# A fused routed-attention and two-MLP kernel: first transfers spread over two queues, weight steps moved later by slots, a finished row of w3 @ w_out closed in three slots

## The chip, the cores and the metric

One core of one Trainium2 chip. The metric is the device time of one execution in microseconds (us), from several executions of the same program; before the change its median is 868.74 us (3 runs, 865.44 to 872.73).

## The reference, cut to what matters

```python
# attention: B, H, S, D = 2, 8, 768, 64; 16 clusters
q_n, k_n, c_n = each divided by (its norm over D + 1e-6)
q_assign = argmax(einsum('bhsd,hcd->bhsc', q_n, c_n), -1)      # the same for k_assign
scores = where(q_assign == k_assign, q @ k.T / sqrt(D), -1e9)
attn = exp(scores - max(scores)); attn = attn / (sum(attn) + 1e-9)
x = attn @ v                      # -> (1536, 512)
# first MLP, w1 and w2 (512, 1024), w3 (1024, 1024), w_out (1024, 512)
x = (((x @ w1) * (x @ w2)) @ w3) @ w_out
# second MLP, w_in (512, 2048), w_out2 (2048, 512)
out = softplus(x @ w_in) @ w_out2
```

The weights arrive as 64-bit floats. Products are made of three single-precision passes (high part, low part), so that they come out near full precision.

## The kernel before, in words

Attention works on 16 heads in 8 pairs. A head's scores are handled in six **slots**, so that the attention loop has 96 slots, and 10 more in which the last slots are finished. Slot s does, in this order on every engine: `mx_pe(s)`, two matmuls (L597, tile `mb`) for a block of 128 queries, and `mx_red(s)` (L606, VectorE, tile `mn`), which takes their extreme; nine slots later `st_pe` (L627, tile `sb`) and `st_exp` (L634, ScalarE, tile `E`), and one slot later still `av_pe` (L642, tile `avb`). So one row of L606 stands for one slot, and the trace has 96 of them.

Two other pieces of work are threaded through the slots by hand:

- **The preparation of the next pair.** The tables `PE` and `EV` give each step a place relative to the pair's first slot (12 times the pair's number): load q and k (`load_qk`, tile `rawqk`, L198), square them (`norm_sq`; on ScalarE for pairs 0 and 1, on GpSimd from pair 2), fold the squares (`norm_fold`, GpSimd, L263), sum them (`norm_sum`, VectorE, L271), transpose (`t1_pe`, L304), split into high and low parts (`t1_ev`: ScalarE writes `H` at L315, VectorE writes `L` at L316), find the clusters (`sims_*`, `assign`), copy `H` and `L` into the heads' operands `q` and `k` (`t_dma`, L332 to L337, seven transfers for each head on SP's queue), and add the cluster rows (`back_*` gives tile `sg`, which `m_dma`, L419, copies). `H` and `L` have one buffer for the first and one for the second head of a pair, so that the third `t1_ev` of a pair (14 slots before the pair's first) cannot write `H_1` until the transfers out of the last pair's `H_1` (4 slots before that pair's first) have landed.
- **The product w3 @ w_out.** It is made beforehand, in 24 pieces (8 of `w_out`, 16 of `w3`, in two rounds g = 0 and 1). Piece n begins at step 3n, and `w_step(k, kinds)` does everything that is due at step k by the table `WT`: `A` scale (L63), `b` `c` `d` the bit operations that turn 64-bit words into floats (L462, L466, L471), `s` split a piece of `w_out` (tiles `woh`, `wol`), `T` transpose a piece of `w3` (L493), `h` `l` its high and low parts, `m` twelve matmuls (L512), `p` add the first round's result (L520, VectorE; nothing in round 0), `q` write the result (ScalarE, `w3oh`), `e` its low part (VectorE in round 1). `d` also issues the load of a later piece (`w_load`, L81). The counter `wk` is the next step; the 82nd ends the work, and then `feed.load(3)` issues the first three pieces of `w1` and `w2` (tile `w12r`, 512 KB each).

Before the loop, pair 0 is prepared, pair 1 as far as `t1_ev`, and `wk` reaches 14. So slot s does step 14 + s: the last `m` is at slot 62, and `feed.load(3)` stands at the end of slot 67. All loads before the loop are on SP's queue: centroids, q and k of pair 0, three pieces of weights, v of pair 0, then (behind the 14 transfers of `t_dma`) q, k and v of pair 1. Three banks of PSUM (`rbank`) pass between all these steps by `take` and `give`; `ring` has two buffers for `sq`, `sT` and `sg`.

After the loop both MLPs run (L789, L811, L989, L1032); nothing there is touched.

Of the kernel before, what the change touches and what calls it, by code (L numbers as in the profile page):

```python
# [8 lines left out]
F32 = mybir.dt.float32  # L9
# [9 lines left out]
P = 128  # L19
# [3 lines left out]
def f32(ap):  # L23
    return ap.bitcast(F32)
# [3 lines left out]
def fused_kernel(ctx: ExitStack, tc, q, k, v, centroids, w1, w2, w3, wo, w_in, w_o2, out):  # L28
# [6 lines left out]
    nc = tc.nc  # L35
    B, H, S, D = q.shape
# [3 lines left out]
    QC = S // P  # L40
# [9 lines left out]
    def pool(es, name, bufs=1, side="left", space=None):  # L50
        kw = dict(name=name, bufs=bufs, reuse_waits="tile")
        if space is not None:
            kw["space"] = space
        if space != DRAM:
            kw["side"] = side
        return es.enter_context(tc.tile_pool(**kw))
# [15 lines left out]
    dma_in = nc.sync.dma_start  # L72
# [43 lines left out]
            )  # L116
        return outs

    nc.scalar.preload_act_table_set("natural_log_exp_and_others")
    identF = cpool.tile([P, P], F32, name="identF")  # L120
    make_identity(nc, identF)
    identB = cpool.tile([P, P], BF16, name="identB")
# [56 lines left out]
    ap1 = pool(es_prep, "ap1")  # L179
# [8 lines left out]

    QK, QT, KT, V, PR = {}, {}, {}, {}, {}

    def load_qk(pi):
        if pi >= NPAIR:
            return
        b, h0 = divmod(2 * pi, H)
        r = ap1.tile([P, 2, QC, 2, D], F32, tag="rawqk", name=f"rawqk{pi}")
        for ni, src in enumerate((q, k)):
            for j in range(2):
                dma_in(r[:, j, :, ni, :], src[b, h0 + j].rearrange("(p c) d -> p c d", p=P))  # L198
        QK[pi] = r

    def centroid_load():
        PR["cw"] = ap1.tile([P, D], F32, name="cw")
        dma_in(PR["cw"], centroids.rearrange("h c d -> (h c) d"))
# [54 lines left out]
        PR["sq", j] = sq  # L258

    def norm_fold(pi, j):  # L260
        sq = PR["sq", j]
        for w in (32, 16):
            nc.gpsimd.tensor_tensor(  # L263
                out=sq[..., :w], in0=sq[..., :w], in1=sq[..., w : 2 * w], op=ALU.add
            )

    def norm_sum(pi, j):
        if j == 0:
            PR["n"] = ap1.tile([P, 4, QC, 2, 2], F32, tag="nrm", name=f"nrm{pi}")
        w = 16 if pi else D  # L270
        nc.vector.tensor_reduce(  # L271
            out=PR["n"][:, 0, :, :, j], in_=PR["sq", j][..., :w], op=ALU.add, axis=AX.X
        )
# [139 lines left out]
        nc.scalar.activation(sg, PR["bk"][:, :S], AF.Copy, scale=bigcol[:, 0:1])  # L413
        give(PR["bm"])

    def m_dma(pi, j):
        for ni, d in enumerate((QT, KT)):
            o = 64 * ni + 32 * j
            nc.sync.dma_start(f32(d[2 * pi + j][96:, 0, :]), f32(PR["sg"][o : o + 32, :]))  # L419

# [6 lines left out]
    NW = len(wseq)  # L429
# [103 lines left out]
    def w3_end(n):  # L533
# [7 lines left out]

    WT = {
        "o": {0: "Ab", 1: "c", 2: "d", 5: "s"},
        "3": {0: "Ab", 1: "c", 2: "d", 3: "T", 4: "hl", 7: "m", 8: "pq", 9: "e"},
    }
    WF = {
        "A": w_scale, "b": lambda n: w_bits(n, 0), "c": lambda n: w_bits(n, 1),
# [4 lines left out]
    def w_step(k, kinds):  # L552
        for n in range(max(0, k // 3 - 3), min(NW, k // 3 + 1)):
            for x in WT[wseq[n][0]].get(k - 3 * n, ""):
                if x in kinds:
                    WF[x](n)
# [3 lines left out]
    def load_v(pi):  # L560

        if pi < NPAIR:
            b, h0 = divmod(2 * pi, H)
            for j in range(2):
                t = xp.tile([P, QC, 2 * D], F32, tag="x", name=f"v{pi}_{j}")
                nc.gpsimd.memset(t[:, :, D * (1 - j) : D * (2 - j)], 1.0)
                dma_in(
                    t[:, :, D * j : D * j + D], v[b, h0 + j].rearrange("(p c) d -> p c d", p=P)
                )
                V[2 * pi + j] = t  # L570
# [16 lines left out]
    NH = B * H  # L587
    NSLOT = NH * QC
    ML = 9
    AL = 1  # L590
# [90 lines left out]
    def x_norm(u):  # L681
        g, hf = divmod(u, 2)
        b, h = divmod(g, H)
        if b not in XT:
            XT[b] = xp_.tile([P, CC, S], F32, tag="x1", name="xT1")
        rs = slice(D * (h % 2), D * (h % 2) + D)
        cs = slice(hf * HALF, (hf + 1) * HALF)
        nc.gpsimd.tensor_tensor(  # L688
            out=XT[b][rs, h // 2, cs],
            in0=TT.pop(u)[rs], in1=R[g // 2][rs, cs], op=ALU.mult,  # L690
        )
# [138 lines left out]


    WALL = "AbcdsThlmpqe"
    W0 = 14
    wk = [0]

    def w_next(kinds=WALL):
        w_step(wk[0], kinds)
        wk[0] += 1

    with tc.manual_schedule():  # L840
        centroid_load()
        load_qk(0)
        for _ in range(3):
            w_load()
        load_v(0)
        centroid_prep()
        t1_pe(0, 0)
        t1_pe(0, 1)
        t1_ev(0, 0)
        norm_sq(0, 0)  # L850
        t1_ev(0, 1)
        centroid_turn()
        t1_pe(0, 2)
        t1_pe(0, 3)
        t1_ev(0, 2)
        norm_sq(0, 1)
        t1_ev(0, 3)
        t_dma(0, 0)
        t_dma(0, 1)
        load_qk(1)  # L860
        load_v(1)
        norm_sum(0, 0)
        sims_pe(0, 0)
        sims_ev(0, 0)
        norm_sum(0, 1)
        norm_root(0)
        sims_pe(0, 1)
        sims_ev(0, 1)
        w_next()
        norm_rec(0, 0)  # L870
        norm_rec(0, 1)
        simsT_pe(0)
        w_next()
        norm_rec(0, 2)
        w_next()
        assign(0, 0)
        assign(0, 1)
        w_next()
        back_pe(0)
        back_ev(0)  # L880
        m_dma(0, 0)
        m_dma(0, 1)
        for r in range(-20, -2 * QC):
            steps(PE, r + 2 * QC)
            steps(EV, r + 2 * QC)
            if wk[0] < W0:
                w_next()
        while wk[0] < W0:
            w_next()
        for s in range(NSLOT + ML + AL):  # L890
            j = s - ML
            a = j - AL
            if s < NSLOT:
                mx_pe(s)
                mx_red(s)
            if s and s % QC == 0 and s <= NSLOT:
                m_row(s // QC - 1)
            w_step(wk[0], "hlpqe")
            if a > 0 and a % 3 == 0:
                av_ev(a // 3 - 1)  # L900
            steps(PE, s)
            steps(EV, s)
            if 0 <= j < NSLOT:
                st_pe(j)
                st_exp(j)
            w_step(wk[0], "Abcds")
            if 0 <= a:
                av_pe(a)
            w_step(wk[0], "Tm")
            wk[0] += 1  # L910

            for g in range(NH):
                r = s - (ML + AL + QC * g + QC - 1)
                if r in (2, 4, 6):
                    r_ev(g, r // 2 - 1)
                if r == 8:
                    x_norm(2 * g)
                    x_norm(2 * g + 1)
            if wk[0] == NWSTEP:
                feed.load(3)  # L920
                assert s < ML + AL + QC * NH // 2 + QC + 6
            if s == NSLOT + 1:
                feed.take(2)
                taken += 2
# [176 lines left out]
```

## Time and profile before

| what | value |
|---|---|
| median of 3 runs | 868.74 us (865.44 to 872.73) |
| the profiled execution | 863.85 us, of which the span of the core is 862.0 us |
| busy share of the span | TensorE 93%, VectorE 57%, ScalarE 46%, GpSimd 28% |
| granted TensorE clock, mean | 0.976 of full speed |

The span runs from the first to the last instruction; the remaining 1.85 us lie around it. PE is TensorE (PEld its weight loads), DVE is VectorE, ACT is ScalarE, POOL is GpSimd, SP is the engine that only issues transfers. "L606" is line 606 of the kernel before. In a row of the timeline the bracket holds the idle time of the engine ahead of the row and what ended it.

### The profile page before, as it was taken

The numbers are of one execution on the slowest core, as the hardware profiler recorded it, in microseconds if no ns is written. First come the engines' busy times: TensorE is split into PE (matmuls) and PEld (weight loads), VectorE is DVE, ScalarE is ACT, GpSimd is POOL, SyncE is SP. The second block draws the span as 40 slices with busy tenths as digits, with TensorE's granted clock in tenths as the row PEclk, the third lists the DMA queues.
The fourth block names the chain that finished last, engine by engine and source line by source line (L and its number), as shares of the span: only waits on it lengthen the run. The fifth ranks groups of instructions, "written<-read, shape, count | busy, mean of one in ns | idle before, by whom it ended". The sixth has DMA issues, their size and how long they took to land.

```text
span 862.0 us, 10099 instructions
## 1 busy us (share of the span) xinstructions
PE 797.6 (93%) x3553; PEld 634.6 (74%) x3553; DVE 493.4 (57%) x823; ACT 398.0 (46%) x683; POOL 244.6 (28%) x233
## 2 busy tenths in 40 slices
PE   3279999899989799989999999999999999999997
PEld 3167777677868577757888888888877788888886
DVE  6595566676764545547652345563988744454442
ACT  3425455544453344465453334454564644455443
POOL 2340314442414021125411113231444222222222
PEclk9589999999999989999999999999999999999999
DMA  9775446664633825125511113340120010001001
GB/s 224 163 196 128 129 121 155 155 171 107 145 84 81 195 47 124 35 59 169 184 57 41 58 49 127 117 146 1 49 74 1 7 43 1 0 1 49 1 1 49
DMA packets 77827, 76.40 MB, mean 89 GB/s; under 512 B 46416, under 2 KB 62928, under 8 KB 77776
## 3 DMA queue, kind: packets, MB, share of 16 engines
q1 hardware_dynamic: 77776, 75.75, 33.0%
q8 instruction: 28, 0.46, 0.2%
q14 instruction: 23, 0.19, 0.1%
HBM read 50.41 MB, written 3.24 MB: 62 GB/s over the span
## 4 chain that ended last, share of the span: by engine, by line
PE 74%; DVE 10%; DMA 6%; issue 3%; ACT 3%; SPq 2%; POOL 1%; ACTq 0%; POOLq 0%; DVEq 0%
PE avb L642 11%; PE rb L789 8%; PE sb L789 8%; PE sb L627 7%; PE sb L989 6%; PE mb L1032 6%; PE rb L989 5%; PE rb L512 4%; PE mb L811 4%; PE mb L597 3%; PE rb L1032 3%; PE avb L1032 3%; DMA k<-H 2%; PE avb L811 2%; PE rb L811 2%
## 5 line engine op out<-in xcount | busy, mean ns | idle before, releaser
L606 DVE TENSOR_REDUCE mn<-mb 128x1 f32<-128x768 f32 x96 | 91.6, 954 | 104.1 <-PE mb L597 103.8
L642 PE MATMUL avb<-E,v 128*128 128x384 f32 x384 | 141.9, 491 | 0.0
L66 POOL TENSOR_TENSOR u<-u,t 128x512 f32<-128x512 f32 x48 | 68.4, 1426 | 170.8 <-DVE u L1012 166.6
L627 PE MATMUL sb<-q,k 128*128 128x384 f32 (+1 forms) x384 | 90.4, 357 | 20.8 <-ACT E L634 20.8
L634 ACT ACTIVATE E<-sb 128x768 f32<-128x768 f32 x96 | 77.7, 809 | 49.1 <-PE sb L627 48.4
L642 PEld LDWEIGHTS avb<-E,v 128*128 128x128 f32 x384 | 71.9, 192 | 27.7 <-issue 1.2
L627 PEld LDWEIGHTS sb<-q,k 128*128 128x128 f32 (+1 forms) x384 | 66.4, 192 | 28.2 <-ACT E L634 25.9
L597 PE MATMUL mb<-k,q 128*128 128x384 f32 x192 | 67.9, 435 | 13.1 <-DVE mn L606 13.0
L989 PE MATMUL sb<-ys,wh_i 128*128 128x512 f32 x192 | 64.1, 395 | 3.5 <-ACT t L1000 2.3
L989 PE MATMUL rb<-ys,wh_i 128*128 128x512 f32 x192 | 63.4, 392 | 0.0
L789 PE MATMUL rb<-xs,wh 128*128 128x512 f32 x192 | 61.7, 392 | 0.0
L789 PE MATMUL sb<-xs,wh 128*128 128x512 f32 x192 | 61.6, 392 | 0.0
L1002 DVE TENSOR_SCALAR u<-t 128x512 f32<-128x512 f32 x48 | 21.1, 440 | 67.7 <-ACT t L1001 67.7
L597 PEld LDWEIGHTS mb<-k,q 128*128 128x128 f32 x192 | 34.6, 192 | 33.9 <-DVE mn L606 18.6
L66 POOL TENSOR_TENSOR wl_o<-d_o,wh_o 128x512 fp32r<-128x512 f32 x16 | 21.6, 1352 | 120.8 <-ACT wh_o L61 120.8
L69 DVE TENSOR_TENSOR gl<-u,gh 128x512 fp32r<-128x512 f32 x48 | 39.6, 825 | 19.6 <-ACT gh L61 19.2
L688 POOL TENSOR_TENSOR xT<-t,R 64x384 f32<-64x384 f32 x32 | 34.2, 1086 | 50.8 <-DMA R<-rd 50.6
L1011 ACT ACTIVATE u<-u 128x512 f32<-128x512 f32 x48 | 30.4, 633 | 35.7 <-DVE t L1008 35.6
L989 PEld LDWEIGHTS sb<-ys,wh_i 128*128 128x128 f32 x192 | 35.9, 188 | 13.6 <-ACT t L1000 3.4
L989 PEld LDWEIGHTS rb<-ys,wh_i 128*128 128x128 f32 x192 | 36.1, 188 | 8.0
L789 PEld LDWEIGHTS rb<-xs,wh 128*128 128x128 f32 x192 | 36.1, 188 | 7.9
L789 PEld LDWEIGHTS sb<-xs,wh 128*128 128x128 f32 x192 | 36.1, 188 | 7.8
(175 smaller groups left out, 1773.9 us busy)
## 6 DMA issues: line engine op xcount, KB each, us to landing
w3r<-in_moe_w_dram SPq DMA_DIRECT2D x16, 512.0 KB
w12r<-in_moe_w_dram SPq DMA_DIRECT2D x16, 512.0 KB
wir<-in_moe_w_in_dram SPq DMA_DIRECT2D x16, 512.0 KB
wor<-in_moe_w_out_dram SPq DMA_DIRECT2D x16, 512.0 KB
q<-H SPq DMA_DIRECT2D x16, 384.0 KB
w3r<-in_moe_w_out_dram SPq DMA_DIRECT2D x8, 512.0 KB
rawqk<-in_q_dram SPq DMA_DIRECT2D x16, 192.0 KB
rawqk<-in_k_dram SPq DMA_DIRECT2D x16, 192.0 KB
```

What stands on the lines that cost most here:

```text
L66: nc.gpsimd.tensor_tensor(out=o, in0=i, in1=hi, op=ALU.subtract)
L69: return nc.vector.tensor_tensor(out=o, in0=i, in1=hi, op=ALU.subtract)
L512: nc.tensor.matmul(m, a[:, ks], bb, start=(mc == 0 and x == 0), stop=(mc == NK - 1 and x == 2))
L597: nc.tensor.matmul(mbank[:, hf, :HALF], QT[g][:, 0, c * P : (c + 1) * P], KT[g][:, 0, hf * HALF : (hf + 1) * HALF], start=True, stop=True,)
L606: nc.vector.tensor_reduce(out=MN[g][:, c : c + 1], in_=mbank[:, :, :HALF], op=ALU.min, axis=AX.XY)
L627: nc.tensor.matmul(sbank[:, i, :HALF], KT[g][: P - 31 * n, n, ks], QT[g][: P - 31 * n, n, qs], start=(n == 0), stop=(n == 1),)
L634: nc.scalar.activation(E[j], sbank[:, :, :HALF], AF.Exp, scale=-1.0)
L642: nc.tensor.matmul(avbank[:, :HALF], V[g][:, 2 * kp + i, :], e[:, i, :], start=(kp == 0 and i == 0), stop=(kp == 2 and i == 1),)
L789: nc.tensor.matmul(bk[:, :BLK], a[:, sl], bb, start=(n == 0), stop=(n == 3 * CC - 1))
L811: nc.tensor.matmul(ybank[e][:, :BLK], a[:, es], bb, start=(fc == 0 and n == 0), stop=(fc == NFC - 1 and n == 2),)
L989: nc.tensor.matmul(hbank[(bl * NF2 + fc) % 4][:, :BLK], a[:, sl], bb, start=(n == 0), stop=(n == 3 * CC - 1))
L1032: nc.tensor.matmul(ob, a[:, sl], bb, start=(fc == 0 and n == 0), stop=(fc == NF2 - 1 and n == 2),)
```

## The change

Three edits. (1) The q and k of pair 0 go by head: the first head's on SP's queue ahead of the centroids, the second head's on ScalarE's queue, ahead of ScalarE's table load; q and k of pair 1 and the `m_dma` of pair 0 are issued by ScalarE; v of pairs 0 and 1 are loaded last before the loop; pair 1's squares are no longer folded on GpSimd but summed in full width by VectorE. (2) The decoding before the loop ends at step 12, and no step is done in slots 0 to 5, so that slot s does step 6 + s. (3) `p` and `q` stand at steps 8 and 9 instead of both at 8, and `e` at 10 instead of 9.

```diff
-    nc.scalar.preload_act_table_set("natural_log_exp_and_others")
...
-    def load_qk(pi):
+    def load_qk(pi, js=range(2), dma=dma_in):
...
-        for ni, src in enumerate((q, k)):
-            for j in range(2):
-                dma_in(r[:, j, :, ni, :], src[b, h0 + j].rearrange("(p c) d -> p c d", p=P))
-        QK[pi] = r
+        if js[0] == 0:
+            QK[pi] = ap1.tile([P, 2, QC, 2, D], F32, tag="rawqk", name=f"rawqk{pi}")
+        for j in js:
+            for ni, src in enumerate((q, k)):
+                dma(
+                    QK[pi][:, j, :, ni, :], src[b, h0 + j].rearrange("(p c) d -> p c d", p=P)
+                )
...
     def norm_fold(pi, j):
+        if pi < 2:
+            return
...
-        w = 16 if pi else D
+        w = 16 if pi >= 2 else D
...
-    def m_dma(pi, j):
+    def m_dma(pi, j, dma=dma_in):
...
-            nc.sync.dma_start(f32(d[2 * pi + j][96:, 0, :]), f32(PR["sg"][o : o + 32, :]))
+            dma(f32(d[2 * pi + j][96:, 0, :]), f32(PR["sg"][o : o + 32, :]))
...
-        "3": {0: "Ab", 1: "c", 2: "d", 3: "T", 4: "hl", 7: "m", 8: "pq", 9: "e"},
+        "3": {0: "Ab", 1: "c", 2: "d", 3: "T", 4: "hl", 7: "m", 8: "p", 9: "q", 10: "e"},
...
-    W0 = 14
+    W0 = 12
...
+        act_dma = nc.scalar.dma_start
+        load_qk(0, [0])
+        load_qk(0, [1], act_dma)
+        nc.scalar.preload_act_table_set("natural_log_exp_and_others")
         centroid_load()
-        load_qk(0)
...
-        load_v(0)
...
-        load_qk(1)
-        load_v(1)
...
-        w_next()
+        load_qk(1, dma=act_dma)
...
-        m_dma(0, 0)
-        m_dma(0, 1)
+        m_dma(0, 0, act_dma)
+        m_dma(0, 1, act_dma)
...
-            if wk[0] < W0:
+            if r % 2 == 0:
+                w_next()
                 w_next()
         while wk[0] < W0:
             w_next()
+        load_v(0)
+        load_v(1)
...
-            w_step(wk[0], "hlpqe")
+            weights = s >= QC
+            if weights:
+                w_step(wk[0], "hlpqe")
...
-            w_step(wk[0], "Tm")
-            wk[0] += 1
+            if weights:
+                w_step(wk[0], "Tm")
+                wk[0] += 1
```

(The steps `Abcds` stand under the same condition.) What the instructions look like now at three places:

SP's queue from the program's start, before (`rawqk` is q and k as loaded, `cw` the centroids, `w3r` a piece of weights; a name's last number is a buffer; "waits DMAHW2" is a wait until the last transfer that used that semaphore has landed):

```order
L203 DMA cw<-in_centroids_dram 128x64
L198 DMA rawqk_149<-in_q_dram 128x6x64 x2
L198 DMA rawqk_149<-in_k_dram 128x6x64 x2
L81 DMA w3r_154<-in_moe_w_out_dram 128x1024
L81 DMA w3r_156<-in_moe_w_out_dram 128x1024
L81 DMA w3r_158<-in_moe_w_out_dram 128x1024
L567 DMA v_0_160<-in_v_dram 128x6x64 [waits DMAHW0_49]
L567 DMA v_1_163<-in_v_dram 128x6x64 [waits DMAHW1_49]
L332 DMA q_215<-H_0_178 64x2x768 [waits DMAHW2_49,Activation_49]
```

ScalarE's queue now, behind the eviction of the clusters' scores (`sT`) of pair 0, up to the squares of pair 1 (`sq_0_284`, `sq_1_291`):

```order
L198 DMA rawqk_246<-in_q_dram 128x6x64 [waits DMAHW5_49]
L198 DMA rawqk_246<-in_k_dram 128x6x64 [waits DMAHW7_49]
L198 DMA rawqk_246<-in_q_dram 128x6x64 [waits DMAHW1_49]
L198 DMA rawqk_246<-in_k_dram 128x6x64 [waits DMAHW3_49]
L63 ACTIVATE w3r_154<-w3r_154 128x512
L416 ACTIVATE sg_278<-rb_102,bigcol 128x768 [waits PE_49]
L422 DMA q_209<-sg_278 32x768 [waits DMAHW6_49,Activation_49]
L422 DMA k_210<-sg_278 32x768 [waits DMAHW0_49]
L422 DMA q_219<-sg_278 32x768 [waits DMAHW2_49]
L422 DMA k_220<-sg_278 32x768 [waits DMAHW4_49]
L258 ACTIVATE sq_0_284<-rawqk_246 128x768 [waits DMAHW7_49,DMAHW5_49]
L258 ACTIVATE sq_1_291<-rawqk_246 128x768 [waits DMAHW3_49,DMAHW4_49,DMAHW2_49,DMAHW6_49,DMAHW1_49,DMAHW0_49]
```

Before, none of these transfers was on ScalarE's queue; they stood on SP's, the loads of pair 1 behind all fourteen transfers of `t_dma`. The second square waits for six semaphores: two of its own loads and the four transfers out of `sg`, whose buffer it takes over.

SP's queue around `feed.load(3)`, before (`w12r` is a piece of w1 or w2; the rows behind it are the `m_dma` and `t_dma` of pair 6):

```order
L672 DMA rd_2379<-r_2330 128x6
L81 DMA w12r_0_2381<-in_moe_w_dram 128x4x256
L81 DMA w12r_1_2383<-in_moe_w_dram 128x4x256
L81 DMA w12r_0_2385<-in_moe_w_dram 128x4x256
L419 DMA q_2291<-sg_2365 32x768
L419 DMA k_2292<-sg_2365 32x768
L332 DMA q_2397<-H_1_2113 64x2x768
L333 DMA k_2398<-H_1_2113 64x768
```

and now (the rows behind it are the first head's `t_dma` of pair 7, the last pair):

```order
L675 DMA rd_2523<-r_2470 128x6
L679 DMA R_2411<-rd_2523 64x768
L81 DMA w12r_0_2559<-in_moe_w_dram 128x4x256
L81 DMA w12r_1_2561<-in_moe_w_dram 128x4x256
L81 DMA w12r_0_2563<-in_moe_w_dram 128x4x256
L658 DMA sd_2497<-t_2568 1x384
L335 DMA q_2575<-H_0_2359 64x2x768
L336 DMA k_2576<-H_0_2359 64x768
```

The three loads of `w12r` stood ahead of transfers out of `H_1` that a later write of `H_1` waits for; they now stand behind the last such write.

## Rows read from the trace of the kernel before

**Rows 1.** The page: busy us, share of the span and instructions

```profile
PE 797.6 (93%) x3553; PEld 634.6 (74%) x3553; DVE 493.4 (57%) x823; ACT 398.0 (46%) x683; POOL 244.6 (28%) x233
```

**Rows 2.** Timeline of VectorE: start us, us, what; slots 0, 12, 24, 36, 48, 60, 72

```profile
42.79 0.95 DVE L606 TENSOR_REDUCE mn<-mb 128x1 f32<-128x768 f32 x1
...
78.71 0.96 DVE L606 TENSOR_REDUCE mn<-mb 128x1 f32<-128x768 f32 x1 [2.47 <-PE mb L597]
...
125.02 0.96 DVE L606 TENSOR_REDUCE mn<-mb 128x1 f32<-128x768 f32 x1 [2.16 <-PE mb L597]
...
167.43 0.96 DVE L606 TENSOR_REDUCE mn<-mb 128x1 f32<-128x768 f32 x1 [1.69 <-PE mb L597]
...
213.09 0.96 DVE L606 TENSOR_REDUCE mn<-mb 128x1 f32<-128x768 f32 x1 [2.72 <-PE mb L597]
...
261.54 0.96 DVE L606 TENSOR_REDUCE mn<-mb 128x1 f32<-128x768 f32 x1 [3.38 <-PE mb L597]
...
307.14 0.96 DVE L606 TENSOR_REDUCE mn<-mb 128x1 f32<-128x768 f32 x1 [2.84 <-PE mb L597]
```

**Rows 3.** Timeline: the matmul that waited longest in three stretches, PE

```profile
163.37 1.65 PE L627 MATMUL sb<-q,k 128*128 128x384 f32 x4 [2.72 <-ACT E L634]
...
204.54 0.98 PE L627 MATMUL sb<-q,k 128*128 128x384 f32 x4 [2.07 <-ACT E L634]
...
302.87 1.65 PE L627 MATMUL sb<-q,k 128*128 128x384 f32 x4 [7.26 <-ACT E L634]
```

**Rows 4.** Timeline: what ScalarE waited for ahead of them

```profile
162.04 0.58 ACT L315 ACTIVATE H<-rb,qkcol 128x384 fp32r<-128x384 f32 x1 [3.67 <-DMA k<-H]
...
201.08 0.60 ACT L61 ACTIVATE w3oh<-rb 128x512 fp32r<-128x512 f32 x1 [5.15 <-DVE rb L520]
...
295.23 0.71 ACT L63 ACTIVATE w12r<-w12r 128x512 f32<-128x512 f32 x1 [2.24 <-DMA w12r<-in_moe_w_dram]
...
301.53 0.58 ACT L315 ACTIVATE H<-rb,qkcol 128x384 fp32r<-128x384 f32 x1 [5.60 <-DMA R<-rd]
```

**Rows 5.** Timeline of SP's queue: the issue of feed.load(3)

```profile
285.84 1.74 SPq L81 DMA_DIRECT2D w12r<-in_moe_w_dram  x3
```

**Rows 6.** Chain of waits, 140 to 320 us: start us, us, what

```profile
290.01 8.62 DMA k<-H
```

**Rows 7.** Chain of waits, 0 to 45 us

```profile
16.26 6.35 DMA k<-H
...
22.63 5.18 DMA rawqk<-in_k_dram
```

**Rows 8.** Windows: PE, PEld, DVE, ACT, POOL busy, PEclk, DMA share, GB/s

```profile
20.00:30.00 10.00, 2.85 (x15) 2.34 (x15) 3.19 (x7) 2.27 (x3) 1.08 (x2) 0.50 1.14 223
50.00:60.00 10.00, 7.20 (x28) 5.26 (x27) 9.76 (x16) 1.34 (x3) 6.46 (x7) 0.83 0.61 161
```

**Rows 9.** Timeline of the start: sums of squares, sg, pair 1's second square

```profile
12.98 1.80 DVE L271 TENSOR_REDUCE nrm<-sq 128x12 f32<-128x768 f32 x2
...
22.51 0.90 ACT L413 ACTIVATE sg<-rb,bigcol 128x768 fp32r<-128x768 bf16 x1 [5.60 <-PE rb L407]
...
30.54 0.35 DVE L271 TENSOR_REDUCE nrm<-sq 128x12 f32<-128x192 f32 x1 [7.15 <-POOL sq L263]
...
30.93 0.84 ACT L257 ACTIVATE sq<-rawqk 128x768 f32<-128x768 f32 x1 [1.65 <-DVE nrm L271]
```

**Rows 10.** Tile w3r, 0 to 60 us: duration ns min/median/max, first and last start us

```profile
L462 DVE TENSOR_SCALAR w3r<-w3r x7: 364/421/1208, 14.9 to 55.0; 128x512 int32<-128x512 int32 x7
...
L466 DVE SCALAR_TENSOR_TENSOR w3r<-w3r x7: 629/693/1806, 16.4 to 58.7; 128x512 int32<-128x512 int32 x7
L471 DVE SCALAR_TENSOR_TENSOR w3d<-w3r x6: 628/790/1777, 17.4 to 51.7; 128x512 int32<-128x512 int32 x6
```

**Rows 11.** Chain of waits, 95 to 102 us: TensorE on steps T and m

```profile
96.11 0.44 PE rb L493 x4
...
98.89 2.78 PE rb L512 x12
```

More of the change, by code (lines that the diff above doesn't have):

```diff
@@ L194, in load_qk @@
         b, h0 = divmod(2 * pi, H)
-        r = ap1.tile([P, 2, QC, 2, D], F32, tag="rawqk", name=f"rawqk{pi}")
-        for ni, src in enumerate((q, k)):
-            for j in range(2):
-                dma_in(r[:, j, :, ni, :], src[b, h0 + j].rearrange("(p c) d -> p c d", p=P))
-        QK[pi] = r
+        if js[0] == 0:
[5 more added lines that the diff above has]
+                )
     def centroid_load():
@@ L684, in x_norm @@
         if b not in XT:
+            assert wk[0] > 3 * NW + 4
             XT[b] = xp_.tile([P, CC, S], F32, tag="x1", name="xT1")
@@ L872, in fused_kernel @@
         simsT_pe(0)
-        w_next()
         norm_rec(0, 2)
-        w_next()
+        w_step(0, "b")
         assign(0, 0)
         assign(0, 1)
-        w_next()
+        w_step(0, "A")
+        wk[0] = 1
         back_pe(0)
         back_ev(0)
-        m_dma(0, 0)
-        m_dma(0, 1)
+        m_dma(0, 0, act_dma)
+        m_dma(0, 1, act_dma)
         for r in range(-20, -2 * QC):
@@ L905, in fused_kernel @@
                 st_exp(j)
-            w_step(wk[0], "Abcds")
+            if weights:
+                w_step(wk[0], "Abcds")
             if 0 <= a:
                 av_pe(a)
-            w_step(wk[0], "Tm")
-            wk[0] += 1
+            if weights:
+                w_step(wk[0], "Tm")
+                wk[0] += 1
             for g in range(NH):
@@ L920, in fused_kernel @@
                 feed.load(3)
-                assert s < ML + AL + QC * NH // 2 + QC + 6
             if s == NSLOT + 1:
```

## The prediction, made before the changed kernel was run

> **What bounds the kernel now.** I read the page first: TensorE is busy 93% of the span, no other engine over 57% [rows 1]. So time is won where TensorE stands still, or before it is dense, and work that is only moved from one dense place to another wins nothing. Next I read one row for each slot: the 96 reductions of L606 mark the attention loop, and every twelfth starts a pair [rows 2]. The twelves last 35.92, 46.31, 42.41, 45.66, 48.45 and 45.60 us. What a twelve holds differs mainly by how many of the weights' steps fall into it: one `m` is 2.78 us of TensorE, one `T` 0.44 [rows 11]. By the rule "slot s does step 14 + s", the second twelve holds four of each, the third one `m` and no `T`, the fourth three and four, the fifth four and four, the sixth one `m`. Measured against the second, the third is too long: 46.31 less three `m` and four `T` (10.1) would be 36.2, and it took 42.4. The fourth should be 43.5 and the fifth 46.3; each is 2.1 over. The sixth should be 36.2 and is 9.4 over.
>
> The timeline gives the places of these excesses, each as idle time of a score matmul that waits for an exponential of ScalarE [rows 3], and ScalarE's rows ahead tell why [rows 4]:
> - 163.37 (2.72 idle): the write of `H_1` waited 3.67 for the copies out of `H_1`.
> - 204.54 (2.07), and a second like it 48 us later in the same place of its twelve: step `q` waited for VectorE's `p`, which stood in the same slot, and `H`, the norm's root and `E` queued behind it.
> - 302.87 (7.26): three loads of 512 KB had been issued at 285.84 [rows 5]; a copy out of `H_1` issued behind them took 8.62 us to land [rows 6]. ScalarE waited 2.24 for the loads themselves, which it decodes here, and 5.60 at `H_1`.
>
> In the start the chain of waits goes through transfers up to 27.81 (22.63 and 5.18): copies of pair 0, then q and k of pair 1 [rows 7]. The 16 DMA engines are full there, at 223 GB/s [rows 8]. From there to the first slot at 42.79 [rows 2] it is 15 us of pair 1's preparation and decoding on ScalarE and VectorE.
>
> **The start.** Two v loads (two heads of 768 x 64 floats, 0.39 MB) no longer stand ahead of pair 1's q and k: at 223 GB/s 1.8 us. The last five copies of head 1 (one of 64 and four of 32 rows of 768 floats, 0.59 MB) must wait for semaphores that pair 1's loads use before them: 2.6 us more that come later. So the loads land at about 23.4 instead of 27.8. But a wait is added. ScalarE now issues `m_dma` itself, each row waiting for an earlier copy, and the second square of pair 1 takes over the buffer of `sg`, so that it waits until these four have landed. `sg` was made from 22.51 to 23.41 [rows 9]; 1.9 us of decoding ahead of it on VectorE (0.42, 0.69, 0.79 [rows 10]) comes later now, so it ends at about 21.5. The copies that `m_dma` waits for land at about 23.5, `m_dma` itself (0.39 MB, 1.8 us, and other traffic beside it) at about 26.5. Behind that square stand ScalarE's scale of a piece and all its `H` rows of pair 1, and VectorE waits for those. The square was at 30.93 [rows 9]: 4.4 us earlier. Behind it VectorE gets two full sums of 0.90 for two of 0.35 (+1.1) [rows 9] and loses two rows of a fifth piece (0.42 and 0.69: -1.1) [rows 10]. The folds on GpSimd go too; I cost that at nothing, because ScalarE's and VectorE's own rows fill the time. Some of the 4.4 is lost because the sums now come behind the late square with a scale and two `H` rows between: I take -3.0, with bounds from -1 (only the v loads count, and ScalarE's four issues in its own queue eat half of it) to -5.5 (nothing is lost, and the folds counted). The centroids land later, behind 0.4 MB of q and k, and with them the first `L` rows, which stand behind them on VectorE; up to 1 us of that is hidden by the traffic, which is what the next step waits for.
>
> **The first twelve slots.** They did steps 14 to 25; they now do steps 12 to 17, in slots 6 to 11. VectorE loses two decodings (0.42, 0.69 and 0.79 each, 3.8 us [rows 10]) and three low parts `l`, rows of the same shape, at the 0.63 that is the least of these: 5.7 us. TensorE loses three `m` and three `T`, 9.7 us [rows 11]. VectorE bounds this stretch (9.76 of 10 us busy from 50 to 60, TensorE 7.20 [rows 8]), so its 5.7 counts. Against it: TensorE's granted clock was 0.50 (1.2 of 2.4 GHz) in the thin stretch from 20 to 30 and 0.83 on average from 50 to 60 [rows 8]; with so little work in slots 0 to 8 it will be at the lower level longer, up to slot 10 or so, and the `H_1` wait of slot 10 loses its cover. I take 2.4 back: -3.3, between 0 and -7.
>
> **The later twelves**, from rows 2, 3 and 11, now with step 6 + s from slot 6 on:
> - Second: four `m`, four `T` as before: 0.
> - Third: four `m`, three `T`: as the second was, less 0.4: 45.9, +3.5.
> - Fourth: no `m`, one `T`, an `H_1` wait without cover: as the third was, less one `m`, plus 0.4: 40.1, -5.6.
> - Fifth: four and four without the `q` wait: 46.3, and `e` now stands ahead of `l` on VectorE in the slots of `m`, +0.15 each: 46.9, -1.5.
> - Sixth: four `m`, three `T`, `feed.load(3)` gone behind the last `H_1`: 46.5, +0.9.
> - Seventh: ScalarE's decoding of the third load comes in slot 78, about three slots of 2.6 us behind an issue that took 9.4 us to landing before (285.84 to 295.23 [rows 4, 5]): a wait of about 1 us, between 0 and 3.
> Sum -1.7. The moved steps alone cost the three `m` and `T` that left the first twelve, +9.7; what pays for them is the feed's stall (-9.4) and the two waits of `q` (-4.2). The tail and both MLPs are the same instructions.
>
> **The sum.** -3.0 - 3.3 - 1.7 = -8.0. The profiled execution took 863.85 with a span of 862.0; so it would take 855.9. It lies 4.9 below the median of the runs; for the median I take the same difference, 868.74 - 8.0, and predict 860.7 us, 0.9% less. About 1% is what a measurement of this kernel can tell from no change.
>
> **A rule that speaks against it.** The 16 DMA engines are full from 20 to 30 us, with one queue issuing [rows 8]. The Trainium skill says ("DMA: Bandwidth & Descriptors", section "Issuing engines are not separate DMA queues") that transfers started by different engines run on the same 16 DMA engines and interleave, so that a second queue saves issue time alone. By it, the trace agrees, the start's gain is only in what goes first, and the rival below follows.
>
> **Rivals.**
> - *The second queue frees nothing.* If q and k of pair 1 interleave with all copies of pair 0 rather than go ahead of them, only the v loads drop out: they land at 26.0, the start gives -1, the sum is -6.0: 862.7. For it: full DMA engines; against: the semaphores hold five copies back.
> - *Deferred work is paid in full.* TensorE's slow clock keeps the first twelve as long as it was (0 for -3.3), and the decode in slot 78 waits 3: the sum is -2.7: 866. For it: 0.50 and 0.83 in the clock column; against: VectorE is the busier engine there.
> - *The `H_1` wait comes in every pair.* `m` used to stand in the slot of the last copies, giving them 2.78 us more until `H_1` is written two slots on; it now stands a slot earlier. If these two slots decide, the wait of 163.37, worth 6.2 with the slow clock behind it (42.4 against 36.2), comes in the second, third, fifth and sixth twelve too: +25, sum +17: 885. It decides when the copies land later than `H_1` is due. Against it: the copies start when `sg` is made, three slots ahead, and any three slots hold one `m`; the uncovered case shows only where no `m` is near.
> - *The change does not do what it says*, as far as `p` and `q`: if `q` still waits (a late `p`), 4.2 stays: 865.
>
> **Chances.** The forecast 0.66, with a range of its own from 855 to 865: -14 with the far ends of the start and the first twelve, -4 with the near ones. A little over half of it lies beyond -8.7 us, since these two far ends lie farther out: 0.38 faster, 0.28 same. Second queue 0.10 (0.02 faster), deferred work 0.10, `q` 0.05: else all within 1%. `H_1` in every pair 0.06 and in one or two pairs 0.03: 0.09 slower; I add 0.03, taken from the forecast's near end, for ScalarE standing longer at its own transfers than I can see. Faster 0.40, same 0.48, slower 0.12. The range goes to 850 (more than both far ends need, the later twelves being good for 2 us either way) and to 869 (deferred work, and no gain in the start).
>
> **What would show it.** Slot 0 at 39.8; slot 12 at 72.4; the sixth twelve without an idle time over 3 us; no idle time at `w3oh` in the fifth; a wait of 2 to 3 us at `H_1` in slot 46 and not in 22, 34, 58, 70. The forecast is wrong if slot 0 comes after 42, or if the sum of the twelves is longer than now.

## The result and the profile after

The changed kernel was compared with the kernel before twice. The first comparison gave 858.02 us (median of 4 runs, 856.56 to 859.42) beside 869.74: a ratio of 0.9869 with a 95% interval from 0.9821 to 0.9917. A second one with more rounds gave 857.36 beside 867.66: 0.9880 [0.9846, 0.9913]. The forecast was 860.7, or 8.0 less; the change is worth 10 to 12, somewhat over 1%. The range held it. By the prediction's own line at 8.7 us both medians lie in "faster" (0.40) and not in "same" (0.48), but both intervals reach above 0.99, so that the line isn't clearly crossed.

The first profiled execution of the changed kernel took 859.42 (span 857.6). Its busy shares, beside [rows 1]:

```profile
PE 802.5 (94%) x3553; PEld 637.9 (74%) x3553; DVE 495.6 (58%) x823; ACT 396.4 (46%) x683; POOL 243.6 (28%) x229
```

The same number of matmuls, four instructions fewer on GpSimd (the folds). The reductions of slots 0, 12, 24, 36, 48, 60 and 72 answer to [rows 2]; their line is L609 now (VectorE's timeline):

```profile
43.39 0.95 DVE L609 TENSOR_REDUCE mn<-mb 128x1 f32<-128x768 f32 x1
...
73.05 0.96 DVE L609 TENSOR_REDUCE mn<-mb 128x1 f32<-128x768 f32 x1
...
119.98 0.95 DVE L609 TENSOR_REDUCE mn<-mb 128x1 f32<-128x768 f32 x1
...
166.42 0.96 DVE L609 TENSOR_REDUCE mn<-mb 128x1 f32<-128x768 f32 x1 [0.53 <-PE mb L600]
...
206.83 0.96 DVE L609 TENSOR_REDUCE mn<-mb 128x1 f32<-128x768 f32 x1 [2.24 <-PE mb L600]
...
255.24 0.95 DVE L609 TENSOR_REDUCE mn<-mb 128x1 f32<-128x768 f32 x1
...
301.12 0.96 DVE L609 TENSOR_REDUCE mn<-mb 128x1 f32<-128x768 f32 x1 [0.61 <-PE mb L600]
```

The reader should subtract neighbours and set the differences beside those of [rows 2]. The kernel before was profiled once more (864.9 us of span instead of 862.0), and so was the changed one (855.3 instead of 857.6), so that each place has two readings:

| stretch | before | after | forecast | first pair | second pair |
|---|---|---|---|---|---|
| slot 0 at | 42.79, 43.23 | 43.39, 42.47 | -3.0 | +0.6 | -0.8 |
| 1st twelve | 35.92, 36.49 | 29.66, 29.94 | -3.3 | -6.3 | -6.6 |
| 2nd | 46.31, 46.30 | 46.93, 46.91 | 0 | +0.6 | +0.6 |
| 3rd | 42.41, 42.61 | 46.44, 46.43 | +3.5 | +4.0 | +3.8 |
| 4th | 45.66, 45.68 | 40.41, 39.73 | -5.6 | -5.3 | -6.0 |
| 5th | 48.45, 48.45 | 48.41, 47.60 | -1.5 | 0.0 | -0.9 |
| 6th | 45.60, 45.65 | 45.88, 45.94 | +0.9 | +0.3 | +0.3 |
| 7th | 31.49, 31.47 | 31.81, 32.13 | +1 | +0.3 | +0.7 |

The rest of the span, from slot 84, gave +1.3 in the first pair and -0.9 in the second; the sums are -4.4 and -9.6.

In the start a step of the forecast fails visibly: the prediction named slot 0 after 42 as a sign of being wrong, and it came at 43.39 and 42.47. ScalarE's timeline of the changed kernel:

```profile
22.48 0.90 ACT L416 ACTIVATE sg<-rb,bigcol 128x768 fp32r<-128x768 bf16 x1 [1.65 <-PE rb L410]
23.41 0.62 ACTq L422 DMA_DIRECT2D q<-sg  x1
...
25.42 0.60 ACTq L422 DMA_DIRECT2D k<-sg  x1
26.13 0.84 ACT L258 ACTIVATE sq<-rawqk 128x768 f32<-128x768 f32 x1 [2.75 <-DMA q<-L]
29.66 0.84 ACT L258 ACTIVATE sq<-rawqk 128x768 f32<-128x768 f32 x1 [2.69 <-DMA k<-sg]
```

`sg` comes at 22.48, as before (22.51 in [rows 9]); ScalarE issues the four copies out of it one after the other until 26.02; the last, in the chain of waits, lands only at 29.48:

```profile
25.42 4.06 DMA k<-sg
```

VectorE's timeline has the first row of the assignment, which `sg` waits for:

```profile
17.89 0.57 DVE L386 TENSOR_TENSOR rb<-rb,nrm 128x384 f32<-128x384 f32 x1 [0.24 <-PE rb L373]
```

The second square stood at 30.93 before [rows 9]; it won 1.3 us, not 4.4 (2.6 in the second pair of profiles, 31.35 and 28.75). Of the loads only the first head's came as early as said; the second head's landed about 2.6 us later, as TensorE's transposes of pair 1 show (they start at 27.95 before, and all nine run in one go there):

```profile
23.62 1.51 PE L307 MATMUL rb<-identF,rawqk 128*128 128x128 f32 x6 [1.17 <-DMA rawqk<-in_k_dram]
26.20 0.87 PE L307 MATMUL rb<-identF,rawqk 128*128 128x128 f32 x3 [1.07 <-DMA rawqk<-in_k_dram]
```

A square that came 1.3 or 2.6 us earlier should still bring slot 0 forward. It came 0.6 us later in the first pair and 0.8 earlier in the second, because the way from the second square to slot 0 is longer now: 13.7 us in both profiles, where it was 11.9. The experiments below take this apart.

How far can a single reading of slot 0 be trusted? Five profiled executions (both of the kernel before, and three experiments that change nothing ahead of slot 0) have it at 42.00, 42.79, 43.12, 43.23 and 44.06. Their second square moves with it, from 30.13 to 32.20, and from this square to slot 0 each takes 11.9 us. So the scatter of 2 us lies in the transfers ahead of the square, and the way behind it can be compared closely.

The wait at `H_1` came where it was forecast, in slot 46 (7.31 us instead of 3.85), as ScalarE's and TensorE's timelines show:

```profile
200.61 0.58 ACT L318 ACTIVATE H<-rb,qkcol 128x384 fp32r<-128x384 f32 x1 [3.87 <-DMA k<-H]
```

```profile
201.94 1.65 PE L630 MATMUL sb<-q,k 128*128 128x384 f32 x4 [2.91 <-ACT E L637]
```

From slot 12 to slot 95 this is the one idle time of TensorE over 1.3 us; those of [rows 3] at 163.37, 204.54 and 302.87 have no successor.

### The profile page after: what moved, and what is told of

It is laid out like the page before. It is cut to its first block, busy times and chain, and to the rows that moved or that the text cites. A ratio compares the mean times of both kernels' runs of the same rounds, so it can differ in the third digit from the quotient of the medians.

```text
span 857.6 us, 10092 instructions
## 1 busy us (share of the span) xinstructions
PE 802.5 (94%) x3553; PEld 637.9 (74%) x3553; DVE 495.6 (58%) x823; ACT 396.4 (46%) x683; POOL 243.6 (28%) x229
## 4 chain that ended last, share of the span: by engine, by line
PE 78%; DVE 9%; ACT 3%; SPq 3%; DMA 3%; issue 2%; POOL 1%; ACTq 0%; DVEq 0%; POOLq 0%
PE avb L645 13%; PE rb L793 8%; PE sb L793 8%; PE sb L630 7%; PE sb L999 6%; PE mb L1042 6%; PE rb L999 5%; PE rb L515 5%; PE mb L815 4%; PE mb L600 4%; PE rb L1042 3%; PE avb L1042 3%; PE avb L815 2%; PE rb L815 2%; PE rb L353 2%
## 5 line engine op out<-in xcount | busy, mean ns | idle before, releaser
L609 DVE TENSOR_REDUCE mn<-mb 128x1 f32<-128x768 f32 x96 | 91.8, 956 | 95.4 <-PE mb L600 95.2
L630 PE MATMUL sb<-q,k 128*128 128x384 f32 (+1 forms) x384 | 92.2, 363 | 9.2 <-ACT E L637 9.2
L600 PE MATMUL mb<-k,q 128*128 128x384 f32 x192 | 70.0, 447 | 16.6 <-DVE mn L609 16.1
L333 POOL MEMSET k<- 1x768 f32 x16 | 11.8, 744 | 107.6 <-issue 83.2
```

Source lines behind the costliest of these rows:

```text
L600: nc.tensor.matmul(mbank[:, hf, :HALF], QT[g][:, 0, c * P : (c + 1) * P], KT[g][:, 0, hf * HALF : (hf + 1) * HALF], start=True, stop=True,)
L609: nc.vector.tensor_reduce(out=MN[g][:, c : c + 1], in_=mbank[:, :, :HALF], op=ALU.min, axis=AX.XY)
L630: nc.tensor.matmul(sbank[:, i, :HALF], KT[g][: P - 31 * n, n, ks], QT[g][: P - 31 * n, n, qs], start=(n == 0), stop=(n == 1),)
```

## The experiments

**Each edit alone, and the feed's load alone.** One comparison, 29 runs of the kernel before (median 867.88).

*Only the start* (against the changed kernel):

```diff
-        "3": {0: "Ab", 1: "c", 2: "d", 3: "T", 4: "hl", 7: "m", 8: "p", 9: "q", 10: "e"},
+        "3": {0: "Ab", 1: "c", 2: "d", 3: "T", 4: "hl", 7: "m", 8: "pq", 9: "e"},
...
-    W0 = 12
+    W0 = 14
...
-            weights = s >= QC
+            weights = True
```

> The start's edit alone (the order of the first transfers on two queues, no folds for the first two pairs), with 14 steps ahead of slot 0, steps in every slot and p and q in one slot as before. My theory, from the trace of the whole change (slot 0 at 43.4 there, 42.8 before): the second square of pair 1 waits for transfers in the new order too, so the start gives nothing: slot 0 between 41.8 and 44.0, time within 2 us of before (ratio 0.998 to 1.003). Rival, the prediction's step: slot 0 near 39.8 and 3 us less (0.9965), the missing 3.6 us of the whole change being due to the fewer steps ahead of slot 0.

Measured: 868.33, ratio 1.0003 [0.9984, 1.0023]; slot 0 at 44.13. The start gives nothing that can be told from zero; its second square waits for the copies out of `sg` as in the whole change (2.14 us here), and the way from there to slot 0 is 14.9 us, where the kernel before, with the same 14 steps, has 11.9.

*Only the six slots* (against before):

```diff
-    W0 = 14
+    W0 = 12
...
-            w_step(wk[0], "hlpqe")
+            weights = s >= QC
+            if weights:
+                w_step(wk[0], "hlpqe")
...
-            w_step(wk[0], "Abcds")
+            if weights:
+                w_step(wk[0], "Abcds")
...
-            w_step(wk[0], "Tm")
-            wk[0] += 1
+            if weights:
+                w_step(wk[0], "Tm")
+                wk[0] += 1
...
```

> The six slots without decoding alone (12 steps ahead of slot 0, none in slots 0 to 5; the feed's loads thereby in slot 75 instead of 67). My theory: the first twelve slots lose 6 us (35.9 to 30), the third twelve gains 4, the fourth loses 3 (the q wait of 2 stays), the fifth gains 2, the sixth is as long as before, its 9 us of stall being paid back in moved steps: 3 to 8 us less in the whole (0.991 to 0.9965). Rival 1, deferred work is paid in full: the first twelve no shorter, the whole within 1 us (0.999 to 1.002). Rival 2: the first twelve's gain needs the new start; then slot 12 less slot 0 stays above 34.

Measured: 863.10, ratio 0.9948 [0.9929, 0.9967]. Slot 0 at 41.84, and the first twelve 29.92: the gain doesn't need the new start. The fourth is 39.16, but the fifth and sixth are 50.52 and 48.34, longer than in the whole change. The cause is `q`: in the shifted order it waits for `p` eight times between 210 and 302 us, 3.9 to 5.5 us each on ScalarE, and TensorE shows six idle times of 0.5 to 0.9 there (one of each, in ScalarE's and TensorE's timelines):

```profile
227.18 0.60 ACT L61 ACTIVATE w3oh<-rb 128x512 fp32r<-128x512 f32 x1 [5.45 <-DVE rb L520]
```

```profile
228.53 0.97 PE L627 MATMUL sb<-q,k 128*128 128x384 f32 x4 [0.53 <-ACT E L634]
```

*Only `p` and `q` in two slots* (against before):

```diff
-        "3": {0: "Ab", 1: "c", 2: "d", 3: "T", 4: "hl", 7: "m", 8: "pq", 9: "e"},
+        "3": {0: "Ab", 1: "c", 2: "d", 3: "T", 4: "hl", 7: "m", 8: "p", 9: "q", 10: "e"},
```

> The third edit alone: p in slot 8 of a row's steps, q in 9, e in 10. My theory: the two idle times of 2.07 us at E behind q go, and nothing takes their place: 2 to 4.2 us less (0.995 to 0.998). Rival: the copies out of H_1 or e behind l take it back, and the time is within 1 us (0.999 to 1.001).

Measured: 864.32, ratio 0.9961 [0.9944, 0.9978]: -3.6. Both idle times of 2.07 us [rows 3] are gone, and none over 1.3 us has come for them. In the profile the fourth and fifth twelves are 1.4 and 0.6 us shorter than before (44.25 and 47.82), but the sixth, with the feed's stall, is 1.1 longer (46.73): the 4.1 us of idle time didn't come back one for one.

*Only the feed's third load in slot 75* (against before):

```diff
-            if wk[0] == NWSTEP:
+            if s == 75:
                 feed.load(3)
...
```

> The feed's third load in slot 75 instead of 67, where the second edit puts it, with all steps as before. If the 7.26 us of idle time and the slower slots around it come from the loads ahead of the copies out of H_1, the sixth twelve falls from 45.6 to about 36 to 38 and the whole by 6 to 9 us (0.9895 to 0.993). Rival: the stall only moves to where the loads are decoded, behind slot 78, and the whole falls by less than 3 (above 0.9965).

Measured: 861.17, ratio 0.9927 [0.9904, 0.9950]: -6.7. The sixth twelve took 38.93 instead of 45.60 (VectorE's timeline, slots 60 and 72), the seventh 31.82: the stall went and didn't move.

```profile
263.34 0.96 DVE L606 TENSOR_REDUCE mn<-mb 128x1 f32<-128x768 f32 x1 [3.38 <-PE mb L597]
...
302.27 0.96 DVE L606 TENSOR_REDUCE mn<-mb 128x1 f32<-128x768 f32 x1 [1.21 <-PE mb L597]
```

TensorE's longest idle time there fell from 7.26 [rows 3] to 2.24 (ScalarE still waits 3.52 us for the copies out of `H_1` there):

```profile
299.62 0.97 PE L627 MATMUL sb<-q,k 128*128 128x384 f32 x4 [2.24 <-ACT E L634]
```

**Together, and the start taken apart.** One comparison with 12 runs of before (867.66).

*The whole change again.*

> The whole change once more, to narrow its interval and to see whether the edits add up. Alone they gave 0.0 (start), -4.8 (six slots) and -3.5 (p and q). If they add up: -8.3, a ratio of 0.990 to 0.991. Rival: they help one another (the new start pays where fewer steps stand ahead of slot 0), and the ratio is 0.987, as in the first, short comparison.

Measured: 857.36, ratio 0.9880 [0.9846, 0.9913], -10.3. The interval holds the sum of the edits (0.990) and the first comparison's 0.987; by itself it doesn't decide between them.

*Edits 2 and 3 with the old start* (the kernel before with both short diffs above).

> Edits 2 and 3 with the start of before. If the new start gives nothing in the whole change either: slot 0 near 42, slot 12 near 71.8, a time within 1.5 us of the whole change in this comparison (ratio 0.989 to 0.992). Rival: the new start gives 3 us there, and this one takes 3 us more than the whole change.

Measured: 855.22, ratio 0.9854 [0.9817, 0.9890], -12.4, with slot 0 at 41.62 and slot 12 at 71.84. So the new start adds nothing to the other two edits and may cost 2 us (the intervals overlap). Its rows show why slot 0 comes so early with the old start (ScalarE's and VectorE's timelines):

```profile
30.88 0.84 ACT L257 ACTIVATE sq<-rawqk 128x768 f32<-128x768 f32 x1 [1.64 <-DVE nrm L271]
```

```profile
41.62 0.94 DVE L606 TENSOR_REDUCE mn<-mb 128x1 f32<-128x768 f32 x1
```

The square is 1.2 us later than in the changed kernel (29.66), but from there it takes only 10.7 us to slot 0, with the same 12 steps of decoding, instead of 13.7. Of these 3.0 us VectorE's rows account for 2.9: behind the square stand eight rows of decoding now (7.85 us) instead of five (5.59), and the last sum is in full width (0.94 instead of 0.34).

Edits 2 and 3 alone sum to -8.3; together -12.4. In the profiles, the fourth to sixth twelves are 138.02 with edit 2 alone and 133.32 with both, 4.7 less. In the kernel before `q` waits for `p` eight times as well, but four of the waits are 1.22 us long, and only two stop TensorE (2.07 us each); in the shifted order all eight are long, and edit 3 takes all of them away.

*Four steps of decoding ahead of pair 1's first square, as before* (against the changed kernel):

```diff
         load_qk(1, dma=act_dma)
+        w_next()
...
         simsT_pe(0)
+        w_next()
         norm_rec(0, 2)
-        w_step(0, "b")
+        w_next()
...
-        w_step(0, "A")
-        wk[0] = 1
+        w_next()
...
-            if r % 2 == 0:
-                w_next()
-                w_next()
+            if wk[0] < W0:
+                w_next()
```

> The whole change, but with four steps of decoding ahead of pair 1's first square, as before, instead of one. My theory of why the start gives nothing: three decodings left the time in which VectorE waits for transfers (23 to 27 us) and stand behind the squares now, on the chain to slot 0, a stretched one at 2.7 us each; then slot 0 comes at 40 to 41.5 and the time falls by 1.5 to 3 us against the whole change. Rival: the wait of the second square for the copies out of sg decides (2.69 us); then slot 0 stays at 43 to 44.

Measured: 860.98, ratio 0.9916 [0.9884, 0.9948]; slot 0 at 45.97, 2.6 to 3.5 later than in the whole change. Slot 0 didn't come at 40 to 41.5, as expected, because the second square came 5.4 us later than in the changed kernel. ScalarE's timeline shows the issues of pair 1's loads, the first and the last of four, then its own step of the decoding, `sg`, and the second square:

```profile
15.47 0.57 ACTq L198 DMA_DIRECT2D rawqk<-in_q_dram  x1
...
18.77 1.57 ACTq L198 DMA_DIRECT2D rawqk<-in_k_dram  x1
20.38 1.22 ACT L63 ACTIVATE w3r<-w3r 128x512 f32<-128x512 f32 x2 [4.42 <-issue]
27.22 0.90 ACT L416 ACTIVATE sg<-rb,bigcol 128x768 fp32r<-128x768 bf16 x1 [5.62 <-PE rb L410]
...
35.04 0.84 ACT L258 ACTIVATE sq<-rawqk 128x768 f32<-128x768 f32 x1 [2.92 <-DMA k<-sg]
```

VectorE's decoding waits for that step, and the assignment of pair 0 stands behind it:

```profile
21.07 0.69 DVE L469 SCALAR_TENSOR_TENSOR w3r<-w3r 128x512 int32<-128x512 int32 x1 [5.04 <-ACT w3r L63]
```

The four issues hold ScalarE for 4.9 us. In the whole change only one piece is begun there, in parts that don't wait for it; that is why `sg` stays at 22.5 there. But the theory holds for its own stretch: with five rows of decoding behind the square, as with the old start, it takes 10.9 us from the square to slot 0 instead of 13.7:

```profile
45.97 0.94 DVE L609 TENSOR_REDUCE mn<-mb 128x1 f32<-128x768 f32 x1
```

So the decodings behind the squares cost nearly 3 us; the experiment lost more than that ahead of them.

*`sg` of pair 0 in a buffer of its own* (against the changed kernel):

```diff
-        sg = PR["sg"] = ring.tile([P, S], F32R, tag="w3k", name=f"sg{pi}")
+        sg = PR["sg"] = (
+            ring.tile([P, S], F32R, tag="w3k", name=f"sg{pi}") if pi
+            else ep.tile([P, S], F32R, tag="E", name="sg0")
+        )
```

> The whole change, but sg of pair 0 in a buffer that nothing waits for before slot 0, so that the second square of pair 1 doesn't wait for the four copies out of it. If this wait decides: the square comes at 27.0 instead of 29.66 and slot 0 at 40.7, 2.5 us less in the whole. Rival, my theory of the decodings: the square comes earlier, but the pieces behind it on VectorE and ScalarE stay in the way, and slot 0 comes at 42.5 or later.

Measured: 855.08, ratio 0.9862 [0.9827, 0.9896]. Both squares now run in one go, and slot 0 comes at 40.51, 2.0 to 2.9 earlier than in the whole change (ScalarE's and VectorE's timelines):

```profile
26.07 1.58 ACT L258 ACTIVATE sq<-rawqk 128x768 f32<-128x768 f32 x2 [2.78 <-DMA k<-sg]
```

```profile
40.51 0.95 DVE L612 TENSOR_REDUCE mn<-mb 128x1 f32<-128x768 f32 x1
```

The idle time in the square's row is that in which ScalarE issues the four copies (until 25.96); the second square is no longer held until they land. From it to slot 0 it still takes 13.7 us. So the wait for the copies out of `sg` takes 1.9 to 2.8 us of the start's gain, and the decodings that now stand behind the square take 3.0 more. In the median the two kernels (855.08 and 857.36) aren't separated, and no run has the buffer and the four early steps of decoding at once.

**Where the feed's gain lies now, and two more.** One comparison with 11 runs of before (868.15).

*The kernel before, profiled again.*

> The kernel before, profiled once more, since its first profiled execution took 863.85 where the median of its runs is 868. My theory: the slow part lies in the places where transfers meet (slot 0, slots 70 and 71), so that these differ by 1 to 4 us from the first profile and the dense twelves (second to fifth) by less than 0.5. Rival: the tail and the MLPs differ.

Measured: 866.72, span 864.9. Of the 2.9 us to the first profile, 0.4 lie ahead of slot 0 and 0.6 in the first twelve, at most 0.2 in any later one, -0.5 in slots 84 to 95, and 2.1 behind slot 95: the rival has the larger part. The windows there (columns as in [rows 8]), first profile, then second:

```profile
365.20:395.00 29.80, 26.30 (x103) 18.16 (x103) 12.53 (x21) 17.04 (x27) 11.32 (x9) 1.00 0.31 89
```

```profile
366.00:395.80 29.80, 25.65 (x94) 17.54 (x93) 10.65 (x19) 16.87 (x27) 9.63 (x8) 0.94 0.24 71
```

TensorE's granted clock is 1.00 in the one and 0.94 in the other, behind the same kind of idle times (1.96 and 1.53 us in the first, 1.97 and 2.17 in the second); cut into stretches of 2.5 us, the second shows 0.57 and 0.75 from 386.0 to 391.0, behind the last of them, that is in part the lower of the two levels (1.2 of 2.4 GHz), and 1.00 in the others. The changed kernel's windows there are at 0.94 in both profiles, with 95 matmuls in the first and 101 in the second. Behind slot 95, where nothing was changed, the kernel before takes 496.8 and 498.9 us and the changed one 498.7 and 497.2. So of the first pair's difference +1.9 comes from there, and of the second's -1.7. At slot 95 itself the pairs differ by -6.3 and -7.9.

*The whole change with the feed's third load in slot 67 again:*

```diff
-            if wk[0] == NWSTEP:
+            if s == 67:
                 feed.load(3)
```

> The whole change, but with the feed's third load issued in slot 67, as in the kernel before, instead of 75. If the gain of the second edit is that of moving this load (alone: -6.4): the stall at H_1 in slot 70 comes back and the time is 5 to 8 us above the whole change's 857.4. Rival: in the new order of the steps the copies out of H_1 don't meet the loads, and the time stays within 2 us of the whole change.

Measured: 859.40, ratio 0.9902 [0.9880, 0.9924]: 2.0 above the whole change, with overlapping intervals; the sixth twelve is 48.65 instead of 45.94. Neither expectation is met. The loads again stand ahead of copies that ScalarE waits for (SP's and ScalarE's timelines):

```profile
283.42 1.52 SPq L81 DMA_DIRECT2D w12r<-in_moe_w_dram  x3
```

```profile
298.88 0.58 ACT L318 ACTIVATE H<-rb,qkcol 128x384 fp32r<-128x384 f32 x1 [4.47 <-DMA k<-sg]
```

But TensorE's longest idle time in the twelve is 2.35 us, where it was 7.26 [rows 3]:

```profile
294.08 0.97 PE L630 MATMUL sb<-q,k 128*128 128x384 f32 x4 [2.35 <-ACT E L637]
```

The sixth twelve holds four `m` now and held one, so that the moved products can fill the wait; ScalarE's wait is also shorter (4.47, where it was 5.60 [rows 4]), and no run separates the two.

*The kernel before with `p` and `q` in two slots and the load in slot 75, nothing else* (both short diffs above).

> The kernel before with p and q in two slots and the feed's third load in slot 75, but with decoding in every slot and the start of before: what the change gives without its first two edits. If those two give nothing beyond the load's new place: -3.5 - 6.4 = -9.9, a ratio of 0.9875 to 0.9895, beside 0.988 for the whole change. Rival: the six slots without decoding give 3 us of their own (as edits 2 and 3 with the old start had 0.9854); then the ratio is 0.9895 or more.

Measured: 857.46, ratio 0.9881 [0.9856, 0.9906], where the whole change has 0.9880. Its fourth to sixth twelves are 44.23, 47.37 and 40.26. Two edits of a line each do what the whole change does, within the 2 us or so that the intervals leave.

*An attempt to beat it:* `sg` in its own buffer, and

```diff
-        while wk[0] < W0:
+        while wk[0] < W0 - 2:
             w_next()
...
+            if s in (1, 3):
+                w_next()
```

> An attempt to beat the change: sg of pair 0 in its own buffer (slot 0 at 40.5 instead of 42.5 to 43.4), and two of the three decodings that stand together ahead of slot 0 put into slots 1 and 3, where VectorE waits about 1 us a slot for TensorE. Expected: slot 0 at 36 to 38, of which slots 1 to 4 give back 2 us: slot 12 at 68.5 to 69.5 instead of 70.5, 1 to 2 us less than with the buffer alone (855.1). Rival: VectorE's decoding delays the reductions in the thin slots as much as it did ahead of them, and slot 12 stays at 70.5.

Measured: 855.76, ratio 0.9848 [0.9826, 0.9869]; slot 0 at 38.96 and slot 12 at 69.12:

```profile
38.96 0.94 DVE L612 TENSOR_REDUCE mn<-mb 128x1 f32<-128x768 f32 x1
...
69.12 0.96 DVE L612 TENSOR_REDUCE mn<-mb 128x1 f32<-128x768 f32 x1
```

From the second square (26.79) to slot 0 it takes 12.2 us now instead of 13.7: the two decodings taken from there gave 1.5. Slot 12 comes 3.3 to 3.9 earlier than in the whole change, as expected, though slot 0 is not at 36 to 38; in the time this isn't separable from the buffer alone or from edits 2 and 3 with the old start. It is the lowest ratio of all, and its interval overlaps the whole change's.

## Why the prediction was right, and where its steps failed

- **The start, forecast -3.0: failed.** The 27.81 from which the loads were counted is the landing of the third of four loads ([rows 7] starts at 22.63, the third issue), the first head's `k`; in the new order the first head's landed when said and the second head's at about 26.1. That cost nothing yet, since the second square was forecast at 26.5. The step that failed is "so it ends at about 21.5 ... `m_dma` itself ... at about 26.5". `sg` ended at 23.4, since the assignment ahead of it waited on VectorE for TensorE (0.24 us of idle time at its first row, 17.89), so that less decoding there won nothing, and the copies landed at 29.5: ScalarE took 2.6 us to issue four, and the last took 4.06 where I had 1.8 us of bytes and some other traffic. The mechanism, a square that takes over `sg`'s buffer, was named; its price was not read from [rows 7], where transfers take 5 to 6 us at that time. With the wait removed slot 0 came at 40.51, near the 39.8. The way behind the square was forecast well (26.5 to 39.8, 13.3; measured 13.7), but that is 3.0 us more than the old start needs with the same number of steps: the decodings that were moved out of the time of the transfers. So even without the wait the start gives only about 1 us beside the old start with 12 steps, which has slot 0 at 41.62 and 41.84.
- **The first twelve, -3.3: too small by half.** The 5.7 us of VectorE was right: in the two windows of the first twelve its busy time fell from 27.67 to 22.20. The 2.4 "taken back" for the slow clock didn't come. The clock was low in both kernels, at other places (before 0.79, then 1.00; after 0.88, then 0.77, by half twelves); why it cost nothing more here no run shows. The two misses have different causes, and their sum is near zero (+0.6 and -1.1 in the two pairs): that the total came out well is luck in this part.
- **The later twelves, -1.7: right within 1.5 each.** The count of `m` and `T` gave the second to fourth and the sixth to 0.6 us. The fifth has no wait of `q` left, as said, but lost at most 0.9 of the forecast 1.5: in the first profile TensorE is busy 47.95 of its 48.41 us.
- **What pays.** "what pays for them is the feed's stall (-9.4) and the two waits of `q` (-4.2)" is borne out in the mechanism: these two without the rest give the whole change's ratio. Alone the stall was worth 6.7 of the 9.4, as 2.24 us of idle time stays, and `p` and `q` 3.6 of the 4.2, of which their two twelves in the profile show 2.0. In the new order the load's place alone is worth only about 2.
- **The rivals.** "The second queue frees nothing" put the loads at 26.0: it is wrong for the first head's (23.62 at the transposes) and right for the second head's (26.20), and the gain went another way. "Deferred work is paid in full" fell with the first twelve at 29.7 to 29.9. "`H_1` in every pair" fell: the wait is in slot 46 alone. `p` and `q` did what they say.
- **From the profile to the median.** The sum was taken as the same difference for the median. At slot 95, the end of what was changed, the two pairs of profiles give -6.3 and -7.9, near the forecast 8.0; the medians give 10 to 12, with intervals from about 7 to 16. Two single executions differ by about 2 us behind slot 95 alone, as the kernel before shows against itself. That the medians differ by more than the profiles do at slot 95 isn't explained.
- **A slip in the range.** The near ends of the start and the first twelve add up to -1 + 0 - 1.7 = -2.7, not to the -4 that the chances use; the result lies far from there.

What stays open: whether the new start costs 2 us or nothing beside edits 2 and 3 (855.22 and 857.36, overlapping intervals), and what it would give with `sg` in its own buffer and the decodings kept ahead of the squares, which no run has together.

## What to carry to other kernels

Before counting a transfer's earlier start as gain, look for what takes over the source's buffer: the time at which the copies out of it have landed, not that at which it was made, is when the next step runs. And look where the work goes that filled the time of the transfers: moved behind them, it stands on the chain (3.0 us here). A wait between two parts of one step can change with the phase of the schedule: two of the waits stopped TensorE before, and six did once another edit had shifted the order. Read a stretch between two rows rather than a single time: slot 0 scattered by 2 us, the way from the second square to it by less than 0.1. When a large rearrangement pays, try its cheapest pieces alone: here the place of one load and one step's split gave all of it.

## What the runs showed that was not expected

ScalarE's four issues of the loads took 0.55 to 1.73 us each in the changed kernel (15.59 to 20.13); with four steps of decoding ahead they took 4.9 us in all (15.47 to 20.34) and held up VectorE by 5.04 us, where a decoding stood behind them. And a decoding row that takes 0.69 us alone took 1.72 beside GpSimd's subtraction (the timelines of GpSimd and VectorE in the changed kernel):

```profile
32.11 1.27 POOL L66 TENSOR_TENSOR wol<-w3d,woh 128x512 fp32r<-128x512 f32 x1 [15.28 <-ACT woh L61]
```

```profile
32.22 1.72 DVE L474 SCALAR_TENSOR_TENSOR w3d<-w3r 128x512 int32<-128x512 int32 x1
```

GpSimd ends at 33.38 and VectorE 0.56 later, nearly its whole length alone. Two more such pairs stand ahead of slot 0 (37.69 and 41.09 on VectorE, 1.64 and 1.59). The Trainium skill says ("SBUF — State Buffer", section "Who interferes with whom") that a VectorE instruction with two inputs from SBUF contends with a GpSimd instruction that reads SBUF, since its second input comes through a read port that they share, and that the order of issue decides which of them is blocked; the trace agrees. Against 0.69 each, the three cost 2.9 us of VectorE's time ahead of slot 0. The kernel before has such rows too (1.78 us at 33.87, beside a GpSimd subtraction at 33.83), so that this is no difference between the two.
